# A Fourier-mixing kernel: the first block's transform returns from DRAM in three groups instead of one

## The chip, the cores and the metric

The program runs on one core of a Trainium2 chip. A core has a matrix engine (TensorE, PE in the profile, its weight loads PEld), VectorE (DVE), ScalarE (ACT), GpSimd (POOL), a queue engine that issues DMAs (SyncE, SP), and 16 DMA engines that all queues share. ScalarE can issue DMAs too, on a queue of its own. The metric is the time of one execution in microseconds (us) on the device, the median of several runs; lower is better.

## The reference

`x` has 8 batches of 3008 x 256 numbers. A Fourier transform runs along both axes and the real part is kept. The 24064 rows of 256 that result pass a two-layer network of 2048 hidden units with the quick GELU. The weights come in 64-bit floating point.

```python
X = np.fft.fft(x, axis=1)
X = np.fft.fft(X, axis=2)
x = X.real.astype(np.float32).reshape(B * S, D)
h = x @ w_in                                   # 256 -> 2048
g = h * (1.0 / (1.0 + np.exp(-1.702 * h)))
out = (g @ w_out).astype(np.float32)           # 2048 -> 256
```

## The kernel before, in words

The length 3008 is 47 x 64. The transform along it has two stages. The first multiplies each of the 64 residues j by a 47-point matrix (32 residues are left after the mirror halves are folded). Its result has 48 rows per residue: a row is numbered 4a + 2u + part, with a from 0 to 11, u and part 0 or 1. The second stage works on tiles whose 128 partitions are (u, part, j), 32 values of j each, with a along the tile. A turn of the layout is needed in between, and it goes through DRAM: the rows are spilled into `Td` and come back ("fill") as `t4t[b]`, 12 tiles of 128 x 256. Stage 2 (line 378) then makes `pq` with VectorE's transposes (line 385), four tiles to a block.

The transform along the 256 columns is folded into `w_in`: `fold_w(n)` multiplies a chunk of 512 columns of `w_in` with `cd` and puts the result in `wcs`. So TensorE does hidden = wcs x pq, the activation, and the product with `w_out`. A step is one (batch, block, half, pair of hidden tiles); a block has 16 of them, eight for each half. The first eight (NP) steps are written out by hand in `SCRIPT`, because the weights are still being prepared. Later steps follow a fixed pattern that keeps TensorE full, in which the next batch is transformed as well.

Weights come as pairs of 32-bit words and are converted on the chip, chunk by chunk: `sizes` (ScalarE or VectorE), `clamp` (GpSimd), `low` (ScalarE), `high` (two VectorE instructions), `finish_in` or `finish_out` (GpSimd), and for some chunks `halved` (VectorE sum and difference, with which `fold_w` takes half the matmuls). Raw chunks share three buffers, so a load waits until the chunk three before it is converted.

The order is written by hand: each engine runs its instructions in the order of the program, and so do the queues of SP and ScalarE. Waits come from what is read and written. DMAs share eight semaphores in turn; an issue may wait for the landing of an older DMA with the same semaphore.

The opening, in the order of the program: `x` is loaded; eight times `mix_first(i)` does two residues and their mirrors on TensorE, and ScalarE copies the result into `made[i // 2]`. After each second one `spill_first` writes rows 0 to 15 of that group to `Td[0]`, with one DMA on SP and one on ScalarE. When all eight spills are down, `fill(0, 0, 4)` loads the four tiles of block 0 with one DMA (line 358). Behind it on SP: the first `w_out` chunk (line 416), the third `w_in` chunk (line 411), and the spills of the other 32 rows. In the meantime `w_in` chunk 1 is converted. Then `fold_w(0)`, `halved(1)`, `rotate` and stage 2 of block 0, `first_row(0)` (a bias row), conversion of the first `w_out` chunk, and `fold_w(1)`, before `SCRIPT` begins with `hidden(0)` (pa and pb, line 549). `rows(t)` makes the sums of a step on VectorE (lines 582, 587, 589), `activate` the activation.

Lines to follow the steps by: 336 spills, 358 fills, 365 rotate, 411 and 416 weight loads, 429 and 431 sizes, 435 clamp, 439 low, 454 and 455 high, 467 finish_in, 475 finish_out, 480 and 481 halved, 501 fold_w with halved, 508 its copies, 552 the copy of pa, 396 the copy of the Nyquist row. Line 191 is a helper that issues TensorE's halves for many callers, told apart by tile. Line 222 loads 47 rows of one end of a later batch, line 199 turns a part of a later batch within DRAM.

Of the kernel before, what the change touches and what calls it, by code (L numbers as in the profile page):

```python
# [27 lines left out]
F32 = mybir.dt.float32  # L28
# [7 lines left out]
NJ = NB // 2  # L36
# [11 lines left out]
def view(ap, offset, *dims):  # L48
    return bass.AP(ap.tensor, ap.offset + offset, [list(d) for d in dims])
# [12 lines left out]
def tables(S, D):  # L62

    assert S == NA * NB and D == 256
    H = D // 2
    ks = np.array([kp(u, a) for a in range(NG) for u in range(NU)])
    s = NB * np.arange(NA)[:, None, None] + np.arange(NB)[None, :, None]
    angle = 2.0 * np.pi * ((s * ks) % S) / S
    cos, sin = np.cos(angle), np.sin(angle)
    w1 = np.zeros((NA, NJ + 3, NG * NU, 2))  # L70
    w1[:, 1:NJ, :, 0], w1[:, 1:NJ, :, 1] = cos[:, 1:NJ], sin[:, 1:NJ]
    e0, o0, e1, o1 = ENDS
    w1[:, e0, :, 0], w1[:, o0, :, 0], w1[:, e1, :, 1], w1[:, o1, :, 1] = cos[:, 0], sin[:, 0], cos[:, NJ], sin[:, NJ]


    w0 = np.zeros((128, NJ + 1, NG * NU, 2))
    low, high, back = w0[0:2 * NA:2], np.zeros((NA, NJ + 1, NG * NU, 2)), NJ - np.arange(1, NJ)
    low[:] = w1[:, :NJ + 1]
    high[:, 1:NJ, :, 0], high[:, 1:NJ, :, 1] = cos[:, NJ + back], -sin[:, NJ + back]
    high[:, e0, :, 1], high[:, o0, :, 1] = cos[:, NJ], -sin[:, NJ]  # L80
    w0[33:33 + 2 * NA:2] = high
    sign = np.ones((128, 4))
    sign[33:33 + 2 * NA:2] = -1.0

    c, q = np.divmod(np.arange(NJ), 16)
    m2 = []
    for jj in np.where(c, 16 + q, np.where(q, 16 - q, 0)), 4 * (q // 2) + 2 * (q % 2) + c:
        j, k2 = jj[:, None], np.arange(NB)[None, :]
        beta = 2.0 * np.pi * ((j * k2) % NB) / NB
        m = np.zeros((NU, 2, NJ, 2, NB))  # L90
        m[:, 0, :, 0], m[:, 1, :, 0] = np.cos(beta), -np.sin(beta)
        m[:, 0, :, 1], m[:, 1, :, 1] = np.sin(beta), np.cos(beta)
        m[:, :, 0, 0] = m[:, :, 0, 1] = np.stack([np.ones(NB), 1.0 - 2.0 * (np.arange(NB) % 2)])
        m2.append(m)
    rot = np.zeros((NU, 2, NJ, NU, 2, NJ))
    for i in range(NU):
        for n in range(NJ):
            rot[i, 0, n, i, 1, n], rot[i, 1, n, i, 0, n] = (1.0, -1.0) if n else (0.0, 0.0)
        rot[i, 0, 0, i, 0, 0] = rot[i, 1, 0, i, 1, 0] = 1.0

    m, d = np.arange(D)[:, None], np.arange(H)[None, :]
    phi = 2.0 * np.pi * ((m * d) % D) / D
    cd = np.stack([np.cos(phi), -np.sin(phi)], 1)
    cd[:, 1, 0] = 1.0 - 2.0 * (np.arange(D) % 2)
    cd = cd.reshape(2, H, 2, NB, 2).transpose(1, 0, 2, 4, 3)
    small = [t.reshape(128, -1) for t in (*m2, rot, cd)]
    pad = 64 - NM
    ends = 2.0 * np.pi * ((NJ * np.arange(NM)[:, None] * ks) % S) / S
    w1 = np.pad(w1[:, :NJ + 1], ((0, NM - NA), (0, 0), (0, 0), (0, 0)))
    w1[:, 0], w1[:, NJ] = 0.0, 0.0  # L110
    for c in range(2):
        w1[c::2, 0, :, c], w1[c::2, NJ, :, c] = np.cos(ends[c::2]), np.sin(ends[c::2])
    w1[NA, 0] *= 0.5
    w1 = np.pad(w1.reshape(NM, -1), ((0, 128 - NM), (0, pad)))
    w0 = np.concatenate([w0.reshape(128, -1), np.zeros((128, pad)), sign], 1)
    return np.concatenate([w0, w1], 1).astype(np.float32), np.concatenate(small, 1).astype(np.float32)
# [3 lines left out]
def kernel(ctx: ExitStack, tc, x, w_in, w_out, tab1, tab2, out):  # L120
# [18 lines left out]
    Xr = [nc.dram_tensor(f"Xr{b}", (NA, NJ, D), F32, kind="Internal").ap() for b in range(B)]  # L139
    Nd = nc.dram_tensor("Nd", (B * NBLK, 512), F32, kind="Internal").ap()  # L140
    Tk = nc.dram_tensor("Tk", (B * NBLK * NF, 1), F32, kind="Internal").ap()
    Td = [nc.dram_tensor(f"Td{b}", (NG * 128, D), F32, kind="Internal").ap() for b in range(B)]

    w1 = const.tile([128, (NJ + 1) * NM + 64 - NM], F32, tag="w1", name="w1")
# [186 lines left out]
        to = 2 - i % 2 * 2  # L331
        nc.scalar.copy(made[i // 2][:, to:to + 2, :].rearrange("p j d -> p (j d)"), ps[:])

    def spill_first(k, m0, m1, engines):
        for c, eng in enumerate(engines):
            eng.dma_start(out=view(Td[0], (NJ * m0 + 16 * c + 12 - 4 * k) * D, [NJ * D, m1 - m0], [1, 4 * D]),
                          in_=made[k][64 * c + m0:64 * c + m1].rearrange("p q d -> p (q d)"))

    def load_matrices():
        for r in range(2):  # L340
            for p0, p1 in ROWS:
                nc.sync.dma_start(out=w1[64 * r + p0:64 * r + p1, :], in_=tab1[p0:p1, n0 + 4:])

    def warm(n):

        ps = bank("warm")
        for _ in range(n):
            nc.tensor.matmul(ps[:], lhsT=wcs[0][:, 0:128], rhs=wcs[0][:, 0:512], start=True, stop=True)

# [3 lines left out]
                          in_=xt[64 * c:64 * c + NM, 4 * q:4 * q + 4, :].rearrange("p q d -> p (q d)"))  # L353

    def fill(b, a0=0, a1=NG):
        if a0 == 0:
            t4t[b] = tp.tile([128, NG, D], F32, tag="t4", name="t4")
        nc.sync.dma_start(out=t4t[b][:, a0:a1, :], in_=Td[b].rearrange("(a p) d -> p a d", p=128)[:, a0:a1, :])

# [117 lines left out]
    def halved(n):  # L477

        s = summed[n] = pre["in", n][0]
        nc.vector.tensor_tensor(s[:, 0:512], wst[n][:, 0], wst[n][:, 1], op=ALU.add)  # L480
        nc.vector.tensor_tensor(s[:, 512:], wst[n][:, 0], wst[n][:, 1], op=ALU.subtract)
# [10 lines left out]
        for out, i0, i1 in ((t1, b12, b11), (t2, b22, t1), (t3, b22, b12), (t4, b21, t2)):  # L492
            nc.gpsimd.tensor_tensor(out, i0, i1, op=ALU.subtract)  # L493

    def fold_w(n):
        ps = [bank("psw") for _ in range(2)]
        for cs in range(2):
            if n in summed:
                for odd_d in range(2):
                    c0 = NB * odd_d  # L500
                    nc.tensor.matmul(ps[cs][c0:c0 + NB], lhsT=cd[:, 0, cs, c0:c0 + NB], rhs=summed[n][:, 512 * odd_d:512 * odd_d + 512],  # L501
                                     start=True, stop=True, skip_group_check=True)
        for i in range(2 if n not in summed else 0):
            for cs in range(2):
                halves(ps[cs][:], cd[:, i, cs, :], wst[n][:, i, :], start=(i == 0), stop=(i == 1))
        for cs in range(2):

            nc.scalar.copy(wcs[cs][:, n * 512:(n + 1) * 512].rearrange("p (f c) -> p f c", f=4),
                           free(ps[cs][:], 0, [1, 4], [4, 128]))
# [342 lines left out]
    n0 = (NJ + 1) * NM + 64 - NM  # L852
    flat = wot[:].rearrange("p w a q n -> p (w a q n)")
    odd, w0 = flat[:, 0:n0], flat[:, 6176:6176 + n0 + 4]
    first = tp.tile([128, NG, D], F32, tag="t4", name="first")
    odds = [first[:, 4 * i:4 * i + 4, :].rearrange("p j (two d) -> p (j two) d", two=2) for i in range(3)]
    rooms = [ring("h").rearrange("p (j d) -> p j d", j=4) for _ in range(4)]
    odds += [rooms[3].rearrange("p j (two d) -> p (j two) d", two=2)]
    made = rooms[:3] + [pqp.tile([128, 4, D], F32, tag="pq", name="e")[:]]
    for i, pair_of in enumerate(((0, 7), (1, 6), (2, 5), (3, 4))):  # L860
        for k, g in enumerate(pair_of):
            room[g] = odds[i][:, 4 * k:4 * k + 4, :]
# [23 lines left out]
    odd_weights(12 * NM, 28 * NM)  # L886
    load_in(0, nc.sync, ((0, 1), (1, 2)))
    nc.sync.dma_start(out=small[:, :CD + 4 * H], in_=tab2[:])
    load_in(1, nc.sync)
    warm(6)  # L890

    in0, in1, out0, in2 = ("in", 0), ("in", 1), ("out", 0), ("in", 2)
# [1 line left out]
    for i, need in enumerate(((0, 7), (1,), (6,), (2,), (5,), (3,), (4,), ())):  # L894
        for g in need:
            fold_first(g)
        mix_first(i)
        if i == 0:
            warm(3)
            spare[:] = spare[5:] + spare[:5]  # L900
        if i % 2:
            spill_first(i // 2, 0, 16, (nc.sync, nc.scalar))
        if i == 3:
            sizes(in0, nc.scalar, 0, 512)
            clamp(in0, 0, 512)
        if i in (4, 7):
            low(in0, 512 * (i // 7), 512)
        if i == 6:
            sizes(in0, nc.vector, 512, 512)
            clamp(in0, 512, 512)  # L910
            for h0 in (0, 512):
                high(in0, h0, 512)
    fill(0, 0, 4)
    load_out(0, nc.sync)
    load_in(2, nc.sync)
    for k in range(4):
        spill_first(k, 16, NM, (nc.sync, nc.sync))
    for h0 in (0, 512):
        finish_in(0, h0, 512)
    prepare(in1)  # L920
# [1 line left out]
    low(in1)  # L922
    for h0 in (0, 512):
        clamp(in1, h0, 512)
    for h0 in (0, 512):
        high(in1, h0, 512)
    for h0 in (0, 512):
        finish_in(1, h0, 512)
    load_out(1, nc.sync)
    fill(0, 4, NG)  # L930
    warm(1)
    fold_w(0)
    halved(1)
    rotate(0, 0, 4, nc.scalar.copy)
    prepare(out0)
    sizes(out0, nc.scalar)
    clamp(out0)
    low(out0)
    stage2(0, 0)
    first_row(0)  # L940
    spare.append(spare.pop(0))
    high(out0)
    load_in(3, nc.sync)
    finish_out(0)
    fold_w(1)

    extra = {}
    PLANS = (((*range(9, 18), 22, 23, 24, 25, 26, 29, 30), (15, 17, 26, 31), 33),
# [23 lines left out]
    for b in range(B):  # L972
# [31 lines left out]
                at(t0 + blk * NF + 10, nyquist, *nxt)  # L1004

    SCRIPT = (
        [(prepare, in2), (low, in2), (nyquist, 0, 0), (rows, 0, ((sizes, in2, nc.vector), (clamp, in2)))],
        [(first_row, 1), (activate, 0), (rows, 1), (high, in2), (finish, in2)],
        [(activate, 1), (rows, 2), (halved, 2)],
        [(product, 0, 0, None), (product, 1, 0, None), (bounds, out1), (activate, 2), (bounds, in3), (rows, 3), (activate, 3),  # L1010
         (fold_w, 2), (high, out1), (finish, out1), (high, in3), (finish, in3)],
        [(first_row, 2), (rotate, 0, 4, NG, nc.scalar.copy), (rows, 4), (halved, 3)],
# [103 lines left out]
```

## Time and profile before

| | us |
|---|---|
| median of 3 runs | 1845.58 (1845.10 to 1847.61) |
| profiled execution, time of its own | 1845.24 |
| profiled execution, span of the instructions | 1843.5 |
| PE / DVE / ACT / POOL busy | 1826.2 / 1479.1 / 1139.4 / 997.7 |
| mean granted TensorE clock | 0.997 |
| chunk 1 of w_in landed (line 439 starts) | 26.40 |
| last spill of rows 0 to 15: issue, length to landing | 24.20, 3.17 |
| fill of block 0: issue, length to landing | 27.50, 4.08 |
| first w_out chunk landed (line 429 starts) | 34.10 |
| hidden(0) starts on PE | 38.15 |
| step 0's first sum on DVE (line 582) | 40.42 |

How to read it: times within the execution count from the first instruction. The page's groups give busy time and mean length of one instruction; a bracket in the timeline is the engine's idle time just before, and what ended it. A DMA share of 1 is all 16 engines busy; it can read a little over 1. The granted clock is TensorE's, 1.00 at full rate. Differences of the whole come from one profiled execution, with some 1.7 us of the time outside the span.

### The profile page before, as it was taken

The numbers are of one execution on the slowest core, as the hardware profiler recorded it, in microseconds if no ns is written. First come the engines' busy times: TensorE is split into PE (matmuls) and PEld (weight loads), VectorE is DVE, ScalarE is ACT, GpSimd is POOL, SyncE is SP. The second block draws the span as 40 slices with busy tenths as digits, with TensorE's granted clock in tenths as the row PEclk, the third lists the DMA queues.
The fourth block names the chain that finished last, engine by engine and source line by source line (L and its number), as shares of the span: only waits on it lengthen the run. The fifth ranks groups of instructions, "written<-read, shape, count | busy, mean of one in ns | idle before, by whom it ended". The sixth has DMA issues, their size and how long they took to land.

```text
span 1843.5 us, 55849 instructions
## 1 busy us (share of the span) xinstructions
PE 1826.2 (99%) x23650; PEld 1398.9 (76%) x23650; DVE 1479.1 (80%) x1930; ACT 1139.4 (62%) x2231; POOL 997.7 (54%) x1068
## 2 busy tenths in 40 slices
PE   8999999999999999999999999999999999999998
PEld 4677777777777777777777777777777877778776
DVE  6888788887888778877888778878888788878874
ACT  4666656666666666666666666666656666556663
POOL 3785555554656546564456644666446654444442
PEclk9999999999999999999999999999999999999999
DMA  8721331114211151211502115020241102100101
GB/s 276 189 70 26 90 65 28 55 32 106 43 48 40 35 112 30 61 35 45 111 13 73 33 50 97 23 72 26 75 74 28 29 26 59 28 19 13 23 19 24
DMA packets 150841, 105.95 MB, mean 57 GB/s; under 512 B 106197, under 2 KB 131799, under 8 KB 150032
## 3 DMA queue, kind: packets, MB, share of 16 engines
q1 hardware_dynamic: 147760, 100.33, 22.6%
q8 instruction: 186, 3.05, 0.7%
q10 hardware_dynamic: 2832, 2.05, 0.5%
q14 instruction: 63, 0.52, 0.1%
HBM read 65.07 MB, written 48.05 MB: 61 GB/s over the span
## 4 chain that ended last, share of the span: by engine, by line
PE 95%; POOL 2%; DMA 1%; DVE 1%; issue 0%; ACT 0%; ACTq 0%; DVEq 0%; POOLq 0%; SPq 0%
PE x L191 35%; PE o L191 26%; PE low L701 25%; PE o L701 4%; PE ps L268 2%; PE ps L378 1%; DMA xt<-in_x_dram 1%; PE po L191 0%; DMA big<-in_moe_w_in_dram 0%; PE psw L501 0%; POOL wo L475 0%; PE pa L191 0%; POOL wo L493 0%; POOL big L632 0%; DMA t<-Td 0%
## 5 line engine op out<-in xcount | busy, mean ns | idle before, releaser
L632 POOL TENSOR_TENSOR big<-big 128x256 f32<-128x256 f32 (+1 forms) x376 | 353.6, 940 | 785.7 <-ACT big L624 672.2
L191 PE MATMUL x<-pq,wcs 128*64 128x256 f32 (+1 forms) x6016 | 768.8, 376 | 1.5 <-ACT g L614 0.9
L191 PE MATMUL o<-big,wo 128*64 128x256 f32 (+1 forms) x4800 | 621.0, 375 | 0.5 <-DVE big L639 0.5
L191 PEld LDWEIGHTS x<-pq,wcs 128*64 128x64 f32 x6016 | 414.1, 137 | 181.4 <-issue 15.6
L614 ACT ACTIVATE g<-x 128x512 f32<-128x512 f32 (+1 forms) x376 | 221.7, 590 | 380.1 <-PE x L191 378.9
L191 PEld LDWEIGHTS o<-big,wo 128*64 128x64 f32 x4800 | 341.8, 137 | 146.8 <-DVE big L639 0.9
L633 POOL TENSOR_TENSOR big<-big 128x256 f32<-128x256 f32 (+1 forms) x376 | 411.2, 1094 | 0.0
L621 DVE TENSOR_TENSOR big<-g,x 128x512 f32<-128x512 f32 (+1 forms) x376 | 250.7, 667 | 183.6 <-ACT big L617 183.4
L602 ACT ACTIVATE x<-nb,af 128x256 f32<-128x256 f32 (+1 forms) x752 | 353.0, 469 | 70.1 <-DVE pq L385 57.0
L701 PE MATMUL low<-big 128*64 128x128 f32 (+1 forms) x5888 | 381.4, 270 | 0.0
L701 PEld LDWEIGHTS low<-big 128*64 128x64 f32 x5888 | 336.9, 137 | 28.2
L617 ACT ACTIVATE big<-x 128x512 f32<-128x512 f32 (+1 forms) x376 | 219.2, 583 | 122.2 <-PE x L191 112.2
L663 DVE TENSOR_TENSOR big<-big 128x1024 f32<-128x1024 f32 (+1 forms) x184 | 235.4, 1280 | 65.9 <-PE low L701 43.1
L624 ACT ACTIVATE big<-big 128x512 f32<-128x512 f32 (+1 forms) x376 | 231.6, 616 | 34.9 <-DVE big L621 32.6
L701 PE MATMUL low<-big,wo 128*64 128x128 f32 (+1 forms) x2944 | 220.3, 270 | 0.1
L665 DVE TENSOR_TENSOR big<-big 128x512 f32<-128x512 f32 (+1 forms) x184 | 179.6, 976 | 16.3 <-DVE big L663 0.5
L667 DVE TENSOR_TENSOR big<-big 128x512 f32<-128x512 f32 (+1 forms) x184 | 184.0, 1000 | 0.0
L701 PEld LDWEIGHTS low<-big,wo 128*64 128x64 f32 x2944 | 171.8, 137 | 4.2 <-DVE big L667 0.5
L640 DVE TENSOR_TENSOR big<-big 128x512 f32<-128x512 f32 (+1 forms) x188 | 143.3, 762 | 6.5
L639 DVE TENSOR_TENSOR big<-big 128x512 f32<-128x512 f32 (+1 forms) x188 | 131.2, 698 | 3.5 <-POOL big L632 3.5
L803 DVE TENSOR_TENSOR big<-big,low 128x512 f32<-128x512 f32 (+3 forms) x184 | 109.0, 609 | 3.8
L701 PEld LDWEIGHTS o<-big,wo 128*64 128x64 f32 x1472 | 92.3, 137 | 24.9
(104 smaller groups left out, 1100.5 us busy)
## 6 DMA issues: line engine op xcount, KB each, us to landing
out_dram<-os SPq DMA_DIRECT2D x284, 64.0 KB
t<-Td SPq DMA_DIRECT2D x22, 512.0 KB
Td<-xt SPq DMA_DIRECT2D x56, 192.0 KB
xt<-in_x_dram SPq DMA_DIRECT2D x14, 512.0 KB
xt<-Xr SPq DMA_DIRECT2D x14, 512.0 KB
nb<-Nd SPq DMA_DIRECT2D x23, 256.0 KB
out_dram<-os SPq DMA_DIRECT2D x96, 56.0 KB
Xr<-in_x_dram SPq DMA_DIRECT2D x7, 752.0 KB
```

Source lines behind the costliest of these rows:

```text
L191: nc.tensor.matmul(out[c0:c0 + 64], lhsT=lhs[:, c0:c0 + 64], rhs=rhs, skip_group_check=True, **how)
L602: nc.scalar.activation(x[:, i * 256:i * 256 + n], nbt[b, blk][:, hh * 256:hh * 256 + n], ACTF.Copy, scale=af1[:, f:f + 1])
L614: nc.scalar.activation(two(g[:], n), two(xb[t][:], n), ACTF.Copy, scale=2.0)
L617: nc.scalar.activation(front(t), two(xb[t][:], width(t)), ACTF.Gelu_apprx_sigmoid)
L621: nc.vector.tensor_tensor(back(t), two(gt.pop(t)[:], n), two(xb.pop(t)[:], n), op=ALU.subtract)
L624: nc.scalar.activation(back(t), back(t), ACTF.Gelu_apprx_sigmoid)
L632: eng.tensor_tensor(right(t, S1, n), left(t, A21, n), right(t, A22, n), op=ALU.add)
L633: eng.tensor_tensor(left(t, S3, n), left(t, A11, n), left(t, A21, n), op=ALU.subtract)
L663: nc.vector.tensor_tensor(free(big[:], SUM, *both_), free(big[:], from11 + w, *twice), free(big[:], from11, [at_right(t, 0) + w - from11, ...
L665: nc.vector.tensor_tensor(s2, a11, s1, op=ALU.subtract)
L667: nc.vector.tensor_tensor(s4, a12, s2, op=ALU.subtract)
L701: nc.tensor.matmul(o, lhsT=lhs, rhs=rhs, start=first_in, stop=(p == NP - 2), skip_group_check=True)
```

## The change

The rows of the first transform are renumbered, so that rows 0 to 15 are (u, part) by a rather than a by (u, part); the residues j are interleaved, so that group k of `mix_first` holds every fourth place of j, beginning at PLACE[k]; the host's tables are permuted to match. The spills of rows 0 to 15 go to a DRAM array of their own, `Tf`, as 64 pieces of 1 KB. Block 0 comes back with three DMAs: the odd places after groups 0 and 1 (64 partitions of 4 KB), then those of group 2 and of group 3 (32 partitions each). Both spills of group 2 are on SP. The load of `w_in` chunk 1 moves from SP, ahead of the mixing, to ScalarE's queue after group 2's copies. The spills of the remaining rows of group 0 go ahead of the load of `w_in` chunk 2. Scratch tiles move, so that the target of the fill is free early. Rotate, stage 2 and `first_row(0)` are now ahead of the second half of chunk 1's conversion, of `load_out(1)`, `fill(0, 4, NG)` and `halved(1)`; `fold_w(1)` comes after `hidden(1)` in two fixed banks, `first_row(1)` one step later, and `low` of chunk 2 one step later.

```diff
@@ tables
+    w0[:, :, :16] = w0[:, :, :16].reshape(128, NJ + 1, 4, 4).swapaxes(2, 3).reshape(128, NJ + 1, 16)
...
+    h, y = np.array([0, 2, 1, 3])[np.arange(NJ) % 4], np.arange(NJ) // 4
+    at = 16 * (y // 4) + 4 * h + y % 4
+    for jj in np.where(c, 16 + q, np.where(q, 16 - q, 0))[at], 4 * (q // 2) + 2 * (q % 2) + c:
@@ spills and fills
+    Tf = nc.dram_tensor("Tf", (NJ * 4, 4 * D), F32, kind="Internal").ap()
+    PLACE = 3, 1, 2, 0
-    def spill_first(k, m0, m1, engines):
+    def spill_first(k, engines):
         for c, eng in enumerate(engines):
-            eng.dma_start(out=view(Td[0], (NJ * m0 + 16 * c + 12 - 4 * k) * D, [NJ * D, m1 - m0], [1, 4 * D]),
-                          in_=made[k][64 * c + m0:64 * c + m1].rearrange("p q d -> p (q d)"))
+            eng.dma_start(out=view(Tf, (PLACE[k] + 16 * c) * 16 * D, [D, 16], [64 * D, 4], [1, D]), in_=made[k][64 * c:64 * c + 16])
+    def fill_first(at, apart):
+        one, n = t4t[0][at:at + 1], NJ // apart
+        nc.sync.dma_start(out=bass.AP(one.tensor, one.offset, [[apart * t4t[0][:].ap[0][0], 4 * n], [1, 4 * D]]),
+                          in_=view(Tf, at * 16 * D, [4 * D, 4], [apart * 16 * D, n], [1, 4 * D]))
+    def spill_rest(k):
+        for c in range(2):
+            nc.sync.dma_start(out=view(Td[0], (NJ * 16 + 16 * c + PLACE[k]) * D, [NJ * D, NM - 16], [4 * D, 4], [1, D]),
+                              in_=made[k][64 * c + 16:64 * c + NM])
@@ scratch
-    odds = [first[:, 4 * i:4 * i + 4, :].rearrange("p j (two d) -> p (j two) d", two=2) for i in range(3)]
+    odds = [wcs[1][:, 1024:].rearrange("p (j d) -> p j d", d=H)]
+    odds += [t.rearrange("p j (two d) -> p (j two) d", two=2) for t in (t4t[0][:, 4:8, :], t4t[0][:, 8:12, :], rooms[0])]
@@ opening
-    load_in(1, nc.sync)
...
         if i % 2:
-            spill_first(i // 2, 0, 16, (nc.sync, nc.scalar))
+            spill_first(i // 2, (nc.sync, nc.sync if i == 5 else nc.scalar))
+        if i == 5:
+            load_in(1, nc.scalar)
+        if i == 3:
+            fill_first(1, 2)
+        if i == 7:
+            fill_first(PLACE[2], 4)
...
-    fill(0, 0, 4)
+    fill_first(PLACE[3], 4)
     load_out(0, nc.sync)
+    spill_rest(0)
     load_in(2, nc.sync)
-    for k in range(4):
-        spill_first(k, 16, NM, (nc.sync, nc.sync))
+    for k in range(1, 4):
+        spill_rest(k)
+    spare[:] = ["o2", "o3", "o4", "b2", "b0", "b1"]
...
-    for h0 in (0, 512):
-        high(in1, h0, 512)
-    for h0 in (0, 512):
-        finish_in(1, h0, 512)
-    load_out(1, nc.sync)
-    fill(0, 4, NG)
-    warm(1)
+    high(in1, 0, 512)
+    finish_in(1, 0, 512)
+    warm(1, "o0")
     fold_w(0)
-    halved(1)
     rotate(0, 0, 4, nc.scalar.copy)
+    stage2(0, 0)
+    first_row(0)
     prepare(out0)
     sizes(out0, nc.scalar)
     clamp(out0)
     low(out0)
-    stage2(0, 0)
-    first_row(0)
-    spare.append(spare.pop(0))
+    high(in1, 512, 512)
+    finish_in(1, 512, 512)
+    load_out(1, nc.sync)
+    fill(0, 4, NG)
     high(out0)
+    halved(1)
     load_in(3, nc.sync)
     finish_out(0)
-    fold_w(1)
@@ SCRIPT
-        [(prepare, in2), (low, in2), (nyquist, 0, 0), (rows, 0, ((sizes, in2, nc.vector), (clamp, in2)))],
-        [(first_row, 1), (activate, 0), (rows, 1), (high, in2), (finish, in2)],
-        [(activate, 1), (rows, 2), (halved, 2)],
+        [(nyquist, 0, 0), (prepare, in2), (rows, 0, ((sizes, in2, nc.vector), (clamp, in2)))],
+        [(low, in2), (fold_w, 1, ("o0", "o1")), (activate, 0), (rows, 1), (high, in2), (finish, in2)],
+        [(first_row, 1), (activate, 1), (rows, 2), (halved, 2)],
```

## The prediction

> **What bounds the kernel now.** I read the page's busy shares first: TensorE (PE) is busy for 99% of the span, so the long middle can't be touched by this change, which edits only the opening. Then the chain of waits in the opening, for what stands between the loads and the first dense TensorE work:
>
> ```profile
> 24.20 3.17 DMA Td<-e
> ...
> 27.50 4.08 DMA t<-Td
> 31.59 0.14 issue
> 31.72 0.29 PE psr L191 x4
> 32.01 1.89 PE ps L378 x64
> 33.90 0.95 PE psf L191 x16
> 34.84 3.52 PE psw L501 x8
> 38.36 1.09 PE pa L191 x8
> ```
>
> Columns: start, length, what. The last group's spill takes 3.17 us, the fill of four tiles 4.08, and only then stage 2 and the fold of the second w_in chunk (psw L501) come, ahead of step 0 (pa at 38.15 to 38.36). Next the waits of TensorE over the first 150 us, and the busy time of each engine by stretch (columns: length, busy time of PE, weight loads, VectorE (DVE), ScalarE (ACT), GpSimd (POOL), granted clock, DMA share, GB/s):
>
> ```profile
> PE psr L191 <- DMA t<-Td: 2.6, 1, 2.6
> ...
> PE pb L191 <- DVE big L589: 1.9, 1, 1.9
> ```
>
> ```profile
> 28.45:31.87 3.42, 0.78 (x8) 0.18 (x4) 3.35 (x4) 0.99 (x2) 1.78 (x2) 1.00 0.90 290
> 31.87:35.28 3.41, 3.41 (x86) 2.70 (x86) 2.03 (x6) 1.35 (x3) 1.27 (x1) 0.50 1.00 399
> 35.28:38.69 3.41, 3.41 (x12) 1.06 (x10) 2.60 (x5) 2.00 (x5) 1.20 (x2) 0.50 0.92 340
> 38.69:42.11 3.42, 3.42 (x32) 1.94 (x30) 1.56 (x3) 2.58 (x5) 2.67 (x3) 1.00 0.78 210
> ```
>
> ```profile
> 40.42:61.00 20.58, 18.54 (x184) 12.87 (x180) 19.68 (x29) 14.32 (x22) 10.95 (x8) 1.00 0.73 263
> 62.03:84.00 21.97, 21.97 (x210) 14.60 (x206) 16.92 (x26) 13.72 (x22) 15.48 (x18) 1.00 0.97 205
> ```
>
> Read so: TensorE waits 2.6 us for the transform, then works 6.8 us at half clock. From 40.42 (step 0's first sum, L582) to 61.00 VectorE is the bound, 19.68 busy of 20.58; its end releases TensorE (the 1.9 us wait), which is dense from 62.03. So the number to find is when VectorE starts step 0: before, 8.84 us after the fill lands (40.42 - 31.58). A shift there reaches the end nearly whole.
>
> **How many DMA engines a transfer gets.** The fills change shape, so I looked for transfers alone on the bus (same columns):
>
> ```profile
> 656.50:658.00 1.50, 1.50 (x26) 1.28 (x24) 1.15 (x2) 0.32 (x1) 0.00 (x0) 1.00 0.07 25
> 655.00:655.50 0.50, 0.50 (x10) 0.37 (x8) 0.00 (x0) 0.50 (x3) 0.50 (x2) 1.00 1.09 389
> 1009.80:1010.20 0.40, 0.40 (x10) 0.27 (x6) 0.15 (x1) 0.00 (x0) 0.40 (x1) 1.00 0.10 31
> ```
>
> The first is line 222's load of 47 rows: 25 GB/s and 0.07 of 16 engines, so one engine. The second is a fill of 128 rows: all sixteen. The third is line 199's transfer, whose pattern counts 2 outermost: about two engines. The outermost count, not the size, sets the spread, and an engine gives about 25 GB/s. The new fill's source counts 4 outermost (the (u, part) pairs), its target 64 or 32 partitions. No row has such a pair. Bounds: one engine to sixteen; I take four, nearest to the row with 2. The Trainium skill's page "DMA: Bandwidth & Descriptors" ("Why a DMA increments its semaphore by 16 and not by 1") gives the largest count up to 16 that divides both outermost sizes: by it four, and the sum below stands.
>
> **The change part by part.**
> Tables, the moved scratch tiles, the new bank order and warm(1) on another bank add no instruction: 0. The conversions of chunk 1 are as many halves as before, in another order. Other scratch also frees the fill target early, which only lets the odd fill start before the mixing ends.
>
> Spills: still eight, now 64 pieces of 1 KB instead of 16 of 4 KB. The 1 KB fill ran at 393 GB/s (30.0 to 30.6) and the 8 KB w_out chunk at 422 (31.2 to 33.2), so 7% of 64 KB: under 0.02 us each. The eight spills of the other rows pay the same on 128 KB, 0.02 each, and hold up no load that is due: the next chunk is needed at 47.00 (sizes on ScalarE, no wait there now). One spill of group 2 goes from ScalarE to SP: +0.3 us there, under the wait for its data.
>
> Load of w_in chunk 1: SP loses an issue (0.38 at 18.47); ScalarE gets one in the place of the spill it gave up (0.36 at 22.70), so its copies at 23.10 stay. Without that 1 MB ahead of them the spills of groups 0 and 1 sit right behind the table load (small), for whose landing SP's last spill issue waited 0.8 us, until 23.9: they land at about 24.0, and the odd fill is issued then. If ScalarE had to wait for the table load too (SP's issues often wait for older transfers: 8.7 us in three), its copies would slip 1.1 us, hidden by the next paragraph.
>
> The queue behind the odd fill: on the four engines, from 23.8 (issue at 22.70 plus the 1.06 us from the fill's issue at 27.50 to its first traffic), lie chunk 1's share (1 MB/16 = 64 KB, 2.5 us at 25.5 GB/s), the odd fill's (256 KB/4, 2.5 us) and four spills (0.7 us). SP issues in order, so group 2's spills stand behind the odd fill. They end at 29.5 and land at 30.0 (0.5 us as for the fill: traffic to 31.1, landing 31.58).
>
> The last two fills go at 30.1 and 30.5 (issue 0.38). The old fill's 4.08 us held 512 KB at 393 GB/s, 1.33; fixed part 2.75. Two times 128 KB on four engines is 2.5. Landing: 30.1 + 2.75 + 2.5 = 35.4, which is **+3.8** against 31.58. Bounds for this: sixteen engines give 31.6 (0.0, worked out below); one engine makes the odd fill 10.2 us and the last two as much, landing past 45 (+14).
>
> From landing to step 0: rotate and stage 2 take 2.2 (31.72 to 33.90), transposes 1.43, so 4.0 after landing at best. hidden(0) needs only that, not the 3.66 of fold_w(1): TensorE gains 2.5 relative to the landing. But VectorE now has to do, before step 0's sum, the second half of chunk 1's high words (1.1 to 1.5, rows 28.38 to 29.91), high(out0) (1.92, and not before its clamp on GpSimd, which comes 1.14 + 0.13 + 1.04 after ScalarE's first_row copies at landing + 3.1, so landing + 5.4; GpSimd's finish_in of the second half, 1.3, follows that clamp beside it) and halved(1) (1.37, or 2.2 beside GpSimd as at 50.00). That is landing + 8.8 to 9.6. Before 8.84: **+0.2**, bounds 0 and +0.8. The w_out chunk itself is issued after the fills, lands 2.6 behind them (64 KB an engine at 26 GB/s), before ScalarE is free for it: 0.
>
> Chunk 1 lands near 29 instead of 26.40; its sizes, clamp and first half follow by 32.6, all in the wait for the transform, as do the copies of fold_w(0), which stand behind low(in1) on ScalarE. If the transform were in by 31, they would cost up to 1.5.
>
> fold_w(1) after hidden(1) puts 1.92 us (53.97) into TensorE's stretch between 38.15 and 62.03, where it idled 2.2: covered at full clock. first_row(1) one step later, low(in2) one step later and chunk 2's load two SP issues later (0.8) have slack: rows(2) comes 7 us after rows(0). The next chunks wait on VectorE as before and shift along.
>
> Sum: +3.8 + 0.2 = **+4.0**. On the profiled execution's 1845.24 us (span 1843.5 and 1.7 around it) that is 1849.2; the median of the runs is 0.34 above that execution, so 1849.6. Of this mechanism alone I expect +2.6 (no restart cost in the fixed 2.75) to +5.5.
>
> **The rivals.**
> *Half clock through both steps.* TensorE would now idle from 29.1 to 35.4 and then run small matmuls. The rows above show that a busy stretch of 3.41 us of stage 2 and fold did not lift the clock at 35.28; it rose at 38.69. hidden(0) would start at 39.5; if the clock stays at 0.5 until 45, hidden(0), the Nyquist row and hidden(1) cost 1.72 + 0.86 + 1.72 more on TensorE. Its own path: 35.4 + 4.1 + 21.7 busy + 1.92 = 63.1, with 4.3 more 67.4 against 62.03: **+5.4**, 1851.0. It decides if the clock rises later than about 44. The Trainium skill's page "TensorE: Matmul & The Clock Gate" (Part 1) says that one busy window of about 3.4 us restores full rate: by that the clock is back before hidden(0) and the sum stays +4.0. Here the trace disagrees for one window.
>
> *Sixteen engines for the new fills.* Then the odd fill takes 0.65, the queue empties by 27.6 and lands at 28.1, the last fills go at 28.2 and take 2.75 + 0.65: landing 31.6, no earlier than now, because chunk 1 fills the gap. Total **0 to +0.8**, 1845.9. The 128 targets in all speak for it, the rows with 47 and 2 against.
>
> *Not slower: the transform is back before fold_w(0) ends at 29.08.* If the spills of group 3 overtake chunk 1 and the small fills need no 2.75, TensorE never idles and the clock stays up (row of 84.10: stage 2 in 1.19). Step 0 is then held by the w_out chunk, which stands behind chunk 1 on the engines: 28.0 + 2.5 + 0.5 = 31.0 landing, plus 5.6 to 6.4 for sizes, clamp, high and halved: 37.0, **-3.4**, 1842.2. It decides if the last fill lands by 29.1; that asks for it to be issued at 25, when group 3's copies end only at 24.17.
>
> **How the numbers follow.** Four engines 0.62, half clock 0.15, sixteen 0.13, early transform 0.10. A measurement of this kernel tells 0.2%, 3.7 us, from no change. Of the first case +4.0 lies just above that: 0.41 slower, 0.21 same. Half clock is slower; sixteen same; early transform 0.06 same, 0.04 faster. Sum: slower 0.56, same 0.40, faster 0.04. Range: 1845.0 (the sixteen-engine case) to 1851.4 (half clock); the early transform and the ends stay out.
>
> **What would show it.** Right: the odd fill issued near 24, group 2's spills on SP after it and landing near 30; the DMA share under 0.3 while the last fills run; TensorE waiting 6 us for t; step 0's first sum near 44.4. Wrong: a fill at 0.9 share; t in before 32; step 0 held by anything but halved(1); a clock that doesn't fall.

## The result, and the profile after

The changed kernel took 1852.44 us (median of 6, 1851.92 to 1854.76) beside 1846.66 for the kernel before (median of 6): a ratio of 1.0035 (95% interval 1.0022 to 1.0047). It is slower, as forecast, but by 5.8 us between medians where +4.0 was predicted, and the time lies above the range. The profiled execution took 1852.52 us, its span 1850.7: 7.3 above the profiled execution of before. (That one, 1845.24, was on the quick side: the medians of the kernel before in the later comparisons were 1845.99 to 1846.29.)

The chain of waits after, from the first four spills to step 0 (columns: start, length, what):

```profile
24.55 0.67 SPq L347
...
25.29 0.40 SPq L343
...
25.73 5.19 DMA Tf<-big
...
30.99 0.57 SPq L347
...
31.66 5.27 DMA t<-Tf
...
37.56 1.89 PE ps L394 x64
39.45 0.97 PE psf L196 x16
```

SP issues the odd fill (L347) at 24.55, then group 2's spills (L343), of which the second takes 5.19 us to land. Only then do the last two fills go; the second takes 5.27, so the transform is complete at 36.93 instead of 31.58. The waits of TensorE and the stretches (columns as in the prediction's tables):

```profile
PE psr L196 <- DMA t<-Tf: 8.1, 1, 8.1
```

```profile
28.00:29.00 1.00, 1.00 (x6) 0.14 (x2) 0.27 (x2) 1.00 (x2) 0.84 (x2) 1.00 0.25 102
29.00:30.00 1.00, 0.06 (x2) 0.00 (x0) 0.96 (x2) 0.63 (x2) 0.35 (x1) 1.00 0.25 98
32.00:35.41 3.41, 0.00 (x0) 0.00 (x0) 0.00 (x0) 0.00 (x0) 0.00 (x0) 0.50 0.57 149
35.41:38.82 3.41, 1.65 (x59) 1.66 (x67) 0.00 (x0) 0.17 (x1) 0.00 (x0) 0.50 0.99 327
38.82:42.23 3.41, 3.10 (x48) 2.06 (x34) 2.44 (x6) 1.79 (x4) 0.43 (x1) 0.50 1.01 369
42.23:45.65 3.42, 3.42 (x16) 1.47 (x14) 2.67 (x2) 1.08 (x2) 1.92 (x2) 0.50 1.04 322
48.16:66.90 18.74, 17.94 (x171) 11.85 (x172) 18.01 (x27) 13.14 (x21) 9.61 (x7) 1.00 0.51 182
```

While the odd fill drains, the DMA share is 0.25 and 100 GB/s move: a quarter of the engines at 25 GB/s each. TensorE waits 8.1 us for t and then runs at half clock until 45.65, four windows instead of two. From 48.16 (step 0's first sum, 40.42 before) VectorE is busy 18.01 of 18.74 us, as it was before. The second part of the loss is on VectorE between landing and step 0 (columns: start, length, engine, line, operation, in brackets the idle time ahead):

```profile
42.95 1.75 DVE L470 TENSOR_SCALAR big<-big 128x1024 uint32<-128x1024 uint32 x1 [0.93 <-POOL big L451]
44.73 1.23 DVE L471 SCALAR_TENSOR_TENSOR big<-big 128x1024 uint32<-128x1024 uint32 x1
45.88 0.68 DVE L496 TENSOR_TENSOR big<-wst 128x512 f32<-128x512 f32 x1
46.48 1.76 DVE L497 TENSOR_TENSOR big<-wst 128x512 f32<-128x512 f32 x1
48.16 0.68 DVE L598 TENSOR_TENSOR big<-v,pb 128x512 f32<-128x512 f32 x1
```

The landing is 5.35 later and the way from there to the first sum 11.23 instead of 8.84, +2.39: together +7.74. TensorE's instructions, set against the same ones of before, start 8.0 later from 66 to 800 us and 7.4 later at 1600. So the question for the experiments: which part of the change makes the landing late, and why does the way behind it grow?

### The profile page after: what moved, and what is told of

Its sections match the earlier page's. It is cut to its first block, busy times and chain, and to the rows that moved or that the text cites. A ratio compares the mean times of both kernels' runs of the same rounds, so it can differ in the third digit from the quotient of the medians.

```text
span 1850.7 us, 55846 instructions
## 1 busy us (share of the span) xinstructions
PE 1827.8 (99%) x23650; PEld 1399.4 (76%) x23650; DVE 1481.1 (80%) x1930; ACT 1138.7 (62%) x2231; POOL 997.7 (54%) x1068
## 4 chain that ended last, share of the span: by engine, by line
PE 93%; POOL 2%; DVE 2%; DMA 2%; issue 1%; ACT 0%; SPq 0%; DVEq 0%; POOLq 0%; ACTq 0%
PE x L196 34%; PE o L196 26%; PE low L717 25%; PE o L717 4%; PE ps L273 2%; PE ps L394 1%; DMA xt<-in_x_dram 1%; DMA Tf<-big 1%; POOL wo L491 0%; PE po L196 0%; DMA t<-Tf 0%; DVE big L471 0%; POOL wo L509 0%; POOL wst L483 0%; POOL big L648 0%
```

## The experiments

All but order_alone start from the changed kernel or from one made out of it (one more, warm18, is told of below). The table gives, from each profiled execution, when the transform is complete (landing) and when step 0's first sum starts, and the medians with their ratio to the kernel before, run beside them. Single executions don't open alike: VectorE ends its sums of `x` at 21.3 in those of before and changed, at 22.0 in sixteen, 22.2 in early and merged_warm, and between 21.1 and 21.8 in the others, so a landing can be up to 0.9 later for reasons that lie outside the edit.

| kernel | landing | first sum | between | median us | ratio (95%) |
|---|---|---|---|---|---|
| before | 31.58 | 40.42 | 8.84 | 1845.99 to 1846.66 | 1 |
| changed | 36.93 | 48.16 | 11.23 | 1852.44 | 1.0035 (1.0022, 1.0047) |
| sixteen | 33.07 | 44.66 | 11.59 | 1848.66 | 1.0013 (1.0003, 1.0022) |
| two | 36.07 | 47.3 | 11.2 | 1852.44 | 1.0033 (1.0021, 1.0046) |
| odd_behind | 34.35 | 45.47 | 11.12 | 1849.80 | 1.0019 (1.0010, 1.0029) |
| early | 37.47 | 45.28 | 7.81 | 1849.90 | 1.0021 (1.0011, 1.0030) |
| order_alone | 31.71 | 42.74 | 11.03 | 1847.33 | 1.0007 (0.9998, 1.0016) |
| both | 32.06 | 39.65 | 7.59 | 1845.48 | 0.9999 (0.9990, 1.0008) |
| both_sp | 35.78 | 43.47 | 7.69 | 1848.06 | 1.0009 (1.0000, 1.0018) |
| late_chunk | 33.58 | 43.58 | 10.00 | 1845.76 | 0.9999 (0.9990, 1.0009) |
| merged | 31.68 | 39.24 | 7.56 | 1844.08 | 0.9988 (0.9979, 0.9997) |
| merged_warm | 33.54 | 40.91 | 7.37 | 1844.50 | 0.9992 (0.9983, 1.0001) |

The first sum is the number to go by: in each of these kernels the profiled execution's time moved against that of before as its first sum did, to within 0.7 us (sixteen +4.2 and +3.6, early +4.9 and +4.8, both -0.8 and -0.8, merged -1.2 and -1.2).

**The spread of the fills: sixteen.** `Tf` becomes three arrays, so that a fill's rows lie in the order of its target partitions, in pieces of 1 KB instead of 4; the spills write in that order too (not shown).

```diff
-                          in_=view(Tf, at * 16 * D, [4 * D, 4], [apart * 16 * D, n], [1, 4 * D]))
+                          in_=view(Tf[at], 0, [D, 4 * n], [4 * n * D, 4], [1, D]))
```

> Only the layout of the small array in DRAM changes, so that both sides of each of the three new fills count 64 or 32 outermost; order, queues and bytes stay. Theory A (the fills sit on four engines, and the first one delays what is behind it there): the odd fill no longer holds four engines; group 2's spills land near 28 instead of 30.9, the DMA share stays near 1 until the spills are done, the last two fills are issued near 28 to 28.7 and land near 31.5 to 32 instead of 36.93; the time falls by about 5 us against the changed kernel, to about 1847.5. Rival B (the order of SP's queue, spills behind the odd fill, is what costs): last fills land at 35 or later, time within 2 us of the changed kernel, 1850.5 or more.

The last fills were issued at 29.95 and 30.66 and landed at 33.07: 2.4 us from the second issue, where the changed kernel took 5.27. A had 31.5 to 32 for the landing. The DMA share stayed at 1.00 and 1.02 from 26 to 28 and was down to 0.06 from 29 to 30. The median fell by 3.8, not 5 (by 3.1, if each kernel is set against the kernel before run beside it: +2.7 instead of +5.8). In the profiled execution two things eat the rest: the first four spills, and with them the odd fill, came 0.8 later than in the changed kernel's, and the landing no longer holds step 0. The chain of this kernel:

```profile
31.30 5.82 DMA big<-in_moe_w_out_dram
...
37.13 1.17 ACT big L448
...
38.38 1.05 POOL big L454
...
39.45 1.76 DVE big L473
```

The w_out chunk, which SP issues behind the fills, is now the last to arrive, and its conversion leads into the same VectorE queue. Theory A holds for the landing; B (landing at 35 or later) falls.

**Two outermost counts: two.** A fill's source is written with 2 x 2 in place of 4.

```diff
-                          in_=view(Tf, at * 16 * D, [4 * D, 4], [apart * 16 * D, n], [1, 4 * D]))
+                          in_=view(Tf, at * 16 * D, [8 * D, 2], [4 * D, 2], [apart * 16 * D, n], [1, 4 * D]))
```

> The changed kernel, with the source of each new fill written with 2 as its outermost count instead of 4 (same bytes, same order, same targets). Theory A (the outermost count that both sides share sets the number of engines, an engine gives 25 GB/s): the odd fill takes 5.0 us on two engines instead of 2.5 on four and holds up the spills behind it by 2.5, so the last fills are issued near 33.5, and take 2.5 more themselves: landing near 42 instead of 36.93, DMA share about 0.12 while they run alone, time about +5 us, near 1857. Rival B (the number of engines follows the 32 or 64 targets, or the fills are slow for another reason, as their 4 KB pieces): landing and time as the changed kernel's, within 1 us.

Nothing changed: landing 36.07, the same median, and a DMA share of 0.26 from 28 to 29. That would be B's outcome, but it doesn't decide: planes at 0, 4D, 8D, 12D written as 2 x 2 are the same evenly spaced 4, and SP took the same time for the issues (0.51 to 0.67 us in both). It shows only that how the pattern is written makes no difference where the addresses are the same. So four against sixteen is shown by the share of 0.25 and by the run above; that the outermost count is what decides was not tested further.

**The order on SP's queue: odd_behind.** Still four engines, but the odd fill is issued behind the last spill.

```diff
-        if i == 3:
-            fill_first(1, 2)
         if i == 7:
+            fill_first(1, 2)
             fill_first(PLACE[2], 4)
```

> The changed kernel, with the odd fill issued behind the last spill instead of ahead of group 2's (fills still on four engines, order of the rest as in the changed kernel). Theory A (the odd fill's 2.5 us on four engines stand ahead of the spills, and the last fills wait for those): spills land near 28.2 instead of 30.9, the last fills are issued at 28.4 to 29; the odd fill is now ahead of them on the same engines, so about 0.5 to 1 of the gain is given back: landing 34 to 35 instead of 36.93, time -2 to -3 us. Rival B (nothing is won, since the three fills need 5 us of the same four engines in any order): landing 36 or later, time within 1 us.

```profile
28.84 0.56 SPq L347
...
29.49 4.87 DMA t<-Tf
34.35 0.14 issue
```

As A said: the last fills go at 28.84 and 29.49, landing 34.35, median 2.6 lower. So of the 5.35 about half, 2.6, is spills that stand behind the odd fill. The other 2.8 against the kernel before is a sum of three: the last fills can go 1.3 later (28.84 instead of 27.50, since a spill of group 2 issued behind chunk 1 lands only at 28.82), there is a second one to issue (0.65), and from the last issue to the landing it takes 4.87 instead of 4.08 (0.8).

**The order on VectorE: early and order_alone.** The first undoes the order in the changed kernel, the second makes it in the kernel before, whose spills, first fill and load of chunk 1 stay.

```diff
     fold_w(0)
+    high(in1, 512, 512)
+    finish_in(1, 512, 512)
+    halved(1)
     rotate(0, 0, 4, nc.scalar.copy)
...
     low(out0)
-    high(in1, 512, 512)
-    finish_in(1, 512, 512)
     load_out(1, nc.sync)
     fill(0, 4, NG)
     high(out0)
-    halved(1)
```

> The changed kernel, with the second half of chunk 1's high words, its finish and halved(1) put back ahead of rotate. Theory A (the 2.3 us lost between the fill's landing and step 0 are VectorE's queue, drawn out beside GpSimd): landing stays near 36.9, step 0's first sum comes 8 us behind it, near 44.9 instead of 48.16; the time falls by about 3.3 us, to about 1849. Rival B (TensorE at half clock holds step 0: hidden(0) at 40.7, the Nyquist row at 44.2): first sum at 46.5 or later, time down by at most 1.5 us.

```diff
-    for h0 in (0, 512):
-        high(in1, h0, 512)
-    for h0 in (0, 512):
-        finish_in(1, h0, 512)
-    load_out(1, nc.sync)
-    fill(0, 4, NG)
+    high(in1, 0, 512)
+    finish_in(1, 0, 512)
...
-    halved(1)
...
     first_row(0)
...
+    high(in1, 512, 512)
+    finish_in(1, 512, 512)
+    load_out(1, nc.sync)
+    fill(0, 4, NG)
     high(out0)
+    halved(1)
...
-    fold_w(1)
```

> The kernel before, with the change's order of the opening alone (second half of chunk 1, load_out(1), fill of the rest and halved(1) behind stage 2 and first_row(0); fold_w(1) after hidden(1)); spills, fill and the load of chunk 1 as before. Theory A (the order costs, whatever the transform's landing): landing stays near 31.6, step 0's first sum comes 10.5 to 11.6 behind it, at 42.1 to 43.2 instead of 40.42; time +1.7 to +2.8 us against the kernel before, near 1848.3. Rival B (my prediction's term: 8.8 to 9.6 behind the landing, and what the trace showed came from the late landing): first sum at 40.4 to 41.2, time within 0.8 us of the kernel before.

VectorE in the first, and then in the second (columns as above):

```profile
43.41 0.69 DVE L470 TENSOR_SCALAR big<-big 128x1024 uint32<-128x1024 uint32 x1 [1.88 <-POOL big L451]
44.13 1.23 DVE L471 SCALAR_TENSOR_TENSOR big<-big 128x1024 uint32<-128x1024 uint32 x1
45.28 0.68 DVE L598 TENSOR_TENSOR big<-v,pb 128x512 f32<-128x512 f32 x1
```

```profile
37.52 1.75 DVE L454 TENSOR_SCALAR big<-big 128x1024 uint32<-128x1024 uint32 x1 [0.93 <-POOL big L435]
39.30 1.22 DVE L455 SCALAR_TENSOR_TENSOR big<-big 128x1024 uint32<-128x1024 uint32 x1
40.44 0.68 DVE L480 TENSOR_TENSOR big<-wst 128x512 f32<-128x512 f32 x1
41.04 1.77 DVE L481 TENSOR_TENSOR big<-wst 128x512 f32<-128x512 f32 x1
42.74 0.68 DVE L582 TENSOR_TENSOR big<-v,pb 128x512 f32<-128x512 f32 x1
```

The order costs by itself: with the landing where it was, the first sum moves from 40.42 to 42.74 (A: 42.1 to 43.2), and undone, the way shrinks to 7.81 (A: 8). That is shorter than the 8.84 of before, where the first sum waited 2.06 us for hidden(0), which stood behind fold_w(1): so that move of the change wins about 1 us, as long as VectorE's order doesn't take it back. In time that is +1.2 over the kernel before (A had +1.7 at least; the interval of the ratio reaches from -0.4 to +3.0 us) and 2.5 under the changed kernel (A: 3.3). In A's favour too is where it goes: the same instruction takes 0.69 alone and 1.75 in the change's order, where GpSimd's finish_in of the second half starts just ahead of it:

```profile
42.88 1.26 POOL L483 TENSOR_TENSOR wst<-big 128x512 uint32<-128x512 uint32 x1
```

It ends at 44.14, and VectorE's instruction at 44.70. The Trainium skill's page "SBUF — State Buffer" ("Who interferes with whom") says that VectorE and GpSimd share a pair of ports, which the one that issues first holds for its whole instruction, while the other is blocked; on VectorE's side it names `tensor_scalar` in a two-port mode and instructions with two inputs in SBUF. This trace agrees: L470 began 0.07 us after L483 and ended 0.56 after it.

**The two together: both.** sixteen and early in one kernel.

> The two edits before this one together: fills on sixteen engines, and the second half of chunk 1 and halved(1) ahead of rotate. If the fill's spread and VectorE's order are the two causes and they add: landing near 31.8, first sum near 39.8 to 40.4, time within 1.5 us of the kernel before (1845 to 1847). Rival: the two don't add, since with an early landing the conversion of chunk 1 (landed 27.35) is what VectorE does while t arrives, and stage 2's transposes wait for it: first sum at 42 or later, time about 2 us above the kernel before.

First sum 39.65, median 1845.48, the same as the kernel before: the two causes together are all that the change lost. Medians fall by 3.8 and 2.5 alone and 7.0 together (3.1, 1.9 and 6.3 against the kernel before run beside each, each uncertain by 2 to 3 us), and the first sum comes 3.5 and 2.9 earlier alone and 8.5 together. So they add at least; that it is more together fits the chains, in which each edit alone runs into the next limit, the w_out chunk in sixteen, the late transform in early. The rival, that conversion of chunk 1 ends last in place of the transform, is visible but mild: the chain of this kernel runs from chunk 1's load through its high words and halved(1) to the transposes, which start at 34.57 right behind halved(1).

**Is it the half clock? warm18.** Idle matmuls on TensorE in the wait for t.

```diff
     fold_w(0)
+    warm(18, "o1")
     rotate(0, 0, 4, nc.scalar.copy)
```

> The changed kernel with 18 idle matmuls of 128x512 on TensorE between fold_w(0) and rotate, some 4 to 8 us in the wait for t, whose product nobody reads; no step of the computation is left out. Theory A (VectorE's order binds step 0, the half clock only delays the transform's copies by about 1.2 us): clock 1.00 from 37 on, stage 2 ends 1.2 earlier, first sum 1 to 1.5 earlier, time about -1.2 us. Rival B (the half clock of 13.65 us binds): first sum 3 to 4 us earlier, time -3 to -4. If the matmuls last beyond the landing at 36.93 the gain shrinks by what they overlap.

I had mis-sized it: 18 calls are 36 matmuls of 0.44 us, 15.7 us, and TensorE was still at them long after the landing; 1860.25 us (1.0077, 1.0060 to 1.0093). The time says nothing, but the trace does: with the clock at 1.00 from 30.98 on, the first sum came 10.0 after stage 2's first matmul (48.46 to 58.49), in the changed kernel 11.0 (37.17 to 48.16). The half clock is worth 1.0 us of that way (A: 1.2; B: 3 to 4), since the rest is ScalarE, GpSimd and VectorE. With the order undone there is less room: in early, hidden(0) at half clock ended at 44.93, 0.35 ahead of the first sum.

**A version from these readings: merged.** From both: the odd fill goes behind the last spill, groups 2 and 3 come back in one fill, and halved(1) goes behind stage 2.

```diff
-        if i == 3:
-            fill_first(1, 2)
         if i == 7:
-            fill_first(PLACE[2], 4)
+            fill_first(1, 2)
...
-    fill_first(PLACE[3], 4)
+    fill_first(0, 2)
...
-    halved(1)
     rotate(0, 0, 4, nc.scalar.copy)
     stage2(0, 0)
+    halved(1)
```

> From the kernel with sixteen-engine fills and the early order: SP issues the odd fill behind the last spill, groups 2 and 3 come back in one fill of 64 partitions, and halved(1) goes behind stage 2's transposes. If SP's issues (0.6 to 0.7 each) are what holds the landing at 32.06 there: the last spill is issued near 25 instead of 26.34, the last fill near 28 and lands near 30.8; transposes at 33 instead of 34.57; step 0's first sum near 38.4 instead of 39.65; time about -1.2 us against that kernel, about -1.7 against the one before. Rival: chunk 1, which is ahead of the spills on the engines, holds their landing at 28 and the w_out chunk (35.47 there) holds VectorE's high words: landing above 31.5 or first sum above 39, time within 0.5 us of the one before.

Against the kernel before 0.9988 (0.9979 to 0.9997), 2.2 us less, and 1.4 less than both (1.7, each against the kernel before run beside it): the fastest kernel here, and the gain is close to what a measurement can tell. The landing came at 31.68 (30.8 expected): the spills were issued by 24.87 as hoped, but the last one landed at 28.43, 0.7 after chunk 1 had (27.75), and ScalarE waited for the w_out chunk:

```profile
24.87 3.56 DMA Tf<-e
...
28.58 3.10 DMA t<-Tf
```

```profile
35.07 1.14 ACT L445 ACTIVATE big<-big 128x1024 f32<-128x1024 f32 x1 [0.93 <-DMA big<-in_moe_w_out_dram]
```

So for the trace the rival was the better guess (landing above 31.5, first sum 39.24, above 39), and for the time the theory.

> The same with two idle calls (four matmuls of 0.43 us, whose product nobody reads; no step of the computation is left out) on TensorE between fold_w(0) and rotate, in the wait for t. If the half clock after that wait costs: clock stays 1.00, stage 2 takes 1.2 instead of 1.7 to 2.0, hidden(0) 2.1 instead of 3.9; first sum 1 to 2 us before the version without them, time down as much. If step 0 is held by the w_out chunk's conversion: the same time within 0.5 us. If the clock falls all the same (two calls are 1.75 us of a window of 3.4): the same, or up to 1 us more if they run past the landing.

```diff
+    warm(2, "o1")
     rotate(0, 0, 4, nc.scalar.copy)
```

The clock stayed at 1.00 through the whole opening, and the time is the same: 1844.50 beside 1844.08. Landing to first sum took 7.37 instead of 7.56 (the opening of this execution was 1.9 later as a whole). TensorE had hidden(0) done early and nobody was ready for it, since ScalarE waited for the w_out chunk here too:

```profile
36.69 1.19 ACT L445 ACTIVATE big<-big 128x1024 f32<-128x1024 f32 x1 [0.75 <-DMA big<-in_moe_w_out_dram]
```

**Where chunk 1 stands: both_sp and late_chunk.** In both, chunk 1 goes back to SP ahead of the mixing; in merged, it goes one group later.

```diff
-        if i == 5:
-            load_in(1, nc.scalar)
...
-            spill_first(i // 2, (nc.sync, nc.sync if i == 5 else nc.scalar))
+            spill_first(i // 2, (nc.sync, nc.scalar))
...
+    load_in(1, nc.sync)
     warm(6)
```

> From the kernel with sixteen-engine fills and the early order: w_in chunk 1 goes back to SP ahead of the mixing, and one spill of group 2 back to ScalarE. Theory A (wherever it is issued, chunk 1 is ahead of the last spills on the engines, so the transform can't be back earlier): chunk 1 lands at 26.4, last spills near 27.5 to 28.3, landing 31 to 32; first sum within 0.8 us of 39.65, time within 1 us. Rival B (the later chunk 1 is what makes the groups worth it): the first four spills and with them the odd fill wait behind chunk 1, landing at 33.5 or later and time +1.5 us.

Theory A fell and B held: the time rose by 2.6 us over both. Chunk 1 landed at 27.75 (26.4 expected), the first four spills behind it, so SP issued the odd fill at 28.17 and the spills behind that at 28.95 and 29.56; landing 35.78. The chain shows it:

```profile
18.83 8.92 DMA big<-in_moe_w_in_dram
...
28.95 2.84 DMA Tf<-big
...
31.81 0.61 SPq L350
```

So the move of chunk 1 that the change makes is needed by its groups, and worth 3.7 us of landing in these two executions, of which 0.5 is a later opening.

```diff
-        if i == 5:
+        if i == 7:
             load_in(1, nc.scalar)
```

> The best version so far (fills on sixteen engines, odd fill behind the last spill, groups 2 and 3 in one fill, halved(1) behind stage 2), with the load of chunk 1 one group later, behind group 3's spill on ScalarE's queue. Theory A (chunk 1's 2.5 us lie ahead of the last spills and hold the landing at 31.7): last spills land near 26.5, landing 29.7 to 30.2, chunk 1 lands 1.5 later, near 29; VectorE's chain of chunk 1 then ends 1.5 later and takes the transform's place, so the first sum stays within 0.5 us of 39.24 and the time within 1 us of 1844. Rival B (step 0 follows the landing): first sum 1.5 earlier, time -1.5 us.

The median is 1845.76 (0.9999, 0.9990 to 1.0009), 1.7 over merged: neither theory. ScalarE's sequencer issued chunk 1 at 24.17, ahead of SP's spill of group 3 at 24.69, and that one spill then stood behind the megabyte (24.69 5.54 in the chain), landing 30.23; the last fill came at 33.58. The profiled execution was the slowest of ten (1848.54; its w_out chunk took 8.4 us), so its later times say little. What a chunk 1 behind all spills would do was not tried.

## Why the prediction was right and wrong

*The bound.* Right: a shift of step 0's first sum reaches the end nearly whole (+7.74 there, +8.0 in the middle, +7.4 late, +7.3 in the execution's time), and in all the experiments to within 0.7 us.

*Engines of a transfer.* Right as far as the runs go: 0.25 of the engines at 25 GB/s each. By the Trainium skill's page "DMA: Bandwidth & Descriptors" ("Why a DMA increments its semaphore by 16 and not by 1") the sizes 4 and 64 give four engines; the trace agrees with its 0.25, and rows in target order, 32 and 32 for the last fill, brought it from 5.27 to 2.4 us. The run with a count of 2 couldn't test the rule, and the row that I read as two engines (0.10, 31 GB/s) lies between one and two.

*The failed step, first half: "The last two fills go at 30.1 and 30.5 (issue 0.38). ... Landing: 30.1 + 2.75 + 2.5 = 35.4, which is +3.8."* The mechanism was right, the size was off: 36.93, +5.35. The odd fill was issued at 24.55, not 24.0, and group 2's spills landed at 30.93, not 30.0 (+0.9). SP took 0.57 to 0.67 for an issue of the new fills, not the 0.38 of the old one (+0.3). From the last issue to the landing it took 5.27, not 4.9 (+0.4); what those 0.4 are stays open. odd_behind confirms the queue (2.6 us back from one move), both_sp that chunk 1's place matters.

*The failed step, second half: "That is landing + 8.8 to 9.6. Before 8.84: +0.2, bounds 0 and +0.8."* Measured: 11.23, +2.39, outside my bounds, and 11.03 in order_alone, with no late landing. I had listed the right instructions, and three of them came out dearer. The clamp ended at landing + 6.0, not 5.4: the bias row's matmuls (psf) ended at + 3.5, not 3.1, and ScalarE's two copies (0.24) stood ahead of `sizes`. high(out0), which I had priced as if alone, took 2.93 instead of 1.92, since GpSimd's finish_in runs "beside it", as I wrote myself, and blocks it; halved(1) took 2.28, just over the 2.2 that I gave as its dear end. The row that would have told me stands in the trace of before: L455 at 30.30 took 1.63 there beside GpSimd's finish_in (30.07 to 31.38) and 0.69 without.

```profile
29.23 0.69 DVE L455 SCALAR_TENSOR_TENSOR big<-big 128x512 uint32<-128x512 uint32 x1
...
30.30 1.63 DVE L455 SCALAR_TENSOR_TENSOR big<-big 128x512 uint32<-128x512 uint32 x1
```

*The signs.* The odd fill near 24, group 2's spills behind it (30.93 for 30), the falling clock and a first sum right behind halved(1) came. The DMA share under 0.3 while the last fills run did not: it was 0.23 and 0.42 from 32 to 34, then 0.96 and 0.90 to 36, because SP issues the w_out chunk (32.22) and more spills right behind the fills. TensorE waited 8.1 us, not 6.

*Half clock as a rival.* Its condition came true and its price didn't. The clock stayed at half until 45.65, past the 44 that I named; yet TensorE did not set step 0: with the clock up the way is 1.0 shorter (warm18), and on merged nothing is won (merged_warm). My sum for it, +5.4, is near the measured +5.8 for a wrong reason. The Trainium skill's page "TensorE: Matmul & The Clock Gate" (Part 1) has full rate back after one busy window of about 3.4 us. The traces agree where the window was full of large matmuls (warm18: half from 27.57 to 30.98, TensorE busy 3.41 of it with 128x512 matmuls, then 1.00), and disagree in the window of stage 2 before (31.87 to 35.28, busy 3.41, still half after it).

*Sixteen engines as a rival.* It wasn't this kernel, but as an experiment: I gave 0 to +0.8 with a landing at 31.6; measured was 1.0013, some +2.4, with the landing at 33.07 and VectorE's order in the way behind it; with the order undone, both, -0.5.

*Early transform.* Never near: even merged lands at 31.68, where the last spill landed at 28.43, behind chunk 1 (27.75), and its first sum waits for the w_out chunk's conversion.

*Covers.* fold_w(1), low(in2), first_row(1) at nothing: no run took them out, but both contains all three moves, and its profiled execution is 0.77 us shorter than that of before, with a first sum 0.77 earlier: nothing behind the first sum shows a cost.

*Chances.* "Slower" held, with 0.35% above the 0.2%; the range's upper end was the half-clock case, 1851.4, and both halves erring to the same side carried the time past it. The +5.5 that I gave as the dear end of the whole mechanism does not say what it is made of, and lies inside the range. With every instruction of VectorE's queue priced beside GpSimd (+1.0 on high, +0.9 on halved) on top of it, the end would have been about 1853.0, and the range would have held the result.

## What to carry to other kernels

When a layout is changed so that a transfer comes back in parts, write both sides with the same large outermost count, and look at what stands behind each part in an issuing queue that goes in order: with four engines and a fill ahead of spills the landing came 5.35 us later here. Price an instruction of VectorE that is moved next to GpSimd's by a row where both run, not by its row alone. And ask what arrives next: with the transform in time, a weight chunk was last.

## What the runs showed of the hardware

How exactly VectorE waited for GpSimd. In the five cases looked at (two in the changed kernel, one in merged, two in order_alone), a VectorE instruction that began while GpSimd was in a two-input tensor instruction ended 0.54 to 0.56 us after that one's end, as if only the last half microsecond of it ran: L470 42.95 to 44.70 beside L483 to 44.14, L497 46.48 to 48.24 beside the first L491 to 47.69. An instruction with an operand from the matmul banks (L598, 0.68 at 48.16, in the middle of the second L491) wasn't held. It is a wait for the other's end, not a slower pace, so a price per instruction alone misses it by up to 1.1 us.

The clock fell in the pause and came back late: the changed kernel ran at half clock through windows with 0, 1.65 and 3.10 us busy and through a fourth, in which TensorE was busy for all 3.42, and at 1.00 after that. What lifts it stays open, since in the kernel before a window with 3.41 busy was followed by another at half. With two idle calls in the wait (3.02 busy of 3.41) it stayed at 1.00:

```profile
28.57:31.98 3.41, 3.02 (x14) 0.87 (x11) 1.56 (x3) 2.15 (x3) 1.62 (x3) 1.00 0.33 90
31.98:35.39 3.41, 3.08 (x85) 1.82 (x84) 2.89 (x4) 0.17 (x1) 1.98 (x2) 1.00 0.97 324
```
